# Two attentions in one planned program: input loads, order of the first projections, and the rules of the planner

## The chip, the core and the metric

The kernel runs on one core of a Trainium2 chip. The metric is device time in microseconds (us) of one execution; several executions of the same kernel are compared by their median. One core has five instruction streams that run beside each other and wait for each other by semaphores: TensorE (PE, matmuls; its weight loads are listed apart as PEld), VectorE (DVE), ScalarE (ACT), GpSimd (POOL) and SyncE (SP, which only issues DMAs here). ScalarE and GpSimd issue DMAs too. PE writes its results to PSUM, which has eight banks of 128 partitions x 512 float32.

## The reference

Two attentions over 2048 tokens with 16 heads of 28 numbers; their outputs stand side by side.

```python
def _A_ref(x, wq, wk, wv, wo):          # one key and one value head for all 16 query heads
    q = (x @ wq).reshape(B, S, H, Dh).transpose(0, 2, 1, 3)
    k = x @ wk
    v = x @ wv
    scores = einsum("bhqd,bkd->bhqk", q, k) * Dh ** -0.5
    o = einsum("bhqk,bkd->bhqd", softmax(scores), v)
    return o.transpose(0, 2, 1, 3).reshape(B, S, H * Dh) @ wo

def _B_ref(x, wqkv, wo):                # each query sees 8 keys: itself and 7 before it, two apart
    q, k, v = heads of x @ wqkv
    logits = q . k[pos - 2 * (0..7)] * Dh ** -0.5, masked where the position is below 0
    return (softmax(logits) . v) @ wo

return concatenate([A, B], axis=-1)     # A_x, B_x: 1 x 2048 x 448, all bfloat16
```

Attention A is the large part: 16 heads x 2048 queries x 2048 keys, each score with an exponential.

## The kernel before

**Work.** Queries of A are taken 512 at a time (four chunks `sc`) and heads four at a time (four groups `g`), which makes 16 groups. Keys are taken 128 at a time (16 blocks `tb`). A job is one head's scores of one key block against 512 queries: one matmul (L1512) into one PSUM bank. A group has 16 x 4 = 64 jobs, and A has 1024. Four heads sit in four row strips of the PE array (28 numbers and a row of ones each), so up to four jobs of one batch run side by side.

**Two ways to the exponential.** Most banks go to ScalarE: one ACTIVATE with Exp (L1250) reads two or three neighbouring banks and writes bfloat16 to `P`. The banks 0 to 2 and 3 to 4 are two rings that take turns, so a batch has three or two of these jobs. Other jobs go to VectorE ("D jobs"): a TENSOR_SCALAR (L1560) turns the bank's scores into int16 that, read as bfloat16, are about the exponential; two more steps on VectorE add 32 to it (L1569, `s1`) and 64 to both (L1576, `s2`), which gives four versions whose weighted sum is the exponential more closely. When two such steps of different jobs are ready together, one instruction does both (`pair`, L1206). A D job therefore has four value matmuls (L1624, operand `Z`, with four scaled copies of the values in `vA`) where a ScalarE job has one (operand `P`). The banks 5 to 7 are called flex: they hold D jobs, the running sums of the value matmuls (one bank for each open group) and the projections ("fills").

**Fills.** Everything else on PE is a fill, a list of steps into one flex bank: the first transposes of A's input, projections of keys (`k0` to `k3`), values and queries of A and B, norms of the queries (whose negative half is added as a further row of the score matmul), B's scores and values in 25-query tiles (L1343, L1310), and output projections (all proj at L661). After a fill an eviction is queued, for VectorE or ScalarE.

**The order is made by a planner in Python**, when the program is built. `_Gen.loop` keeps a planned time for each engine, always lets the engine that is furthest behind choose its next instruction, and adds that instruction's planned duration. PE's choice (`pe_choose`) is between the next batch of scores (`do_qk`), value matmuls (`do_pv`), a fill (`fill_pick`: by due time, if its inputs are planned to be there), a filler matmul (`dummy`, L1707 and L1709) and 20 ns of nothing. The result is a fixed list for each engine. On the chip every engine runs its list in order, and waits for semaphores.

The names that the change touches:

- `xA`, `wA` (`plan_start`): the first 512 tokens of A's input go to `xn`, which lies in `P`; 64 partitions by SP's queue and 64 by ScalarE's. Then the query weights (two DMAs) and the value weights (two) go out on ScalarE's queue and the key weights (two) on SP's, which next issues 12 transposing DMAs for the other three token chunks. The dependencies of the query weights are kept under one name, `wq`.
- `FILL0`, `FILLN` (`want_d`): a D job is wanted only while the number of fills done is at least 124 x (jobs done) / 1024 + `FILL0`; also below a share `DRATE` of D jobs.
- `TWOD`, `RINGD`, `RINGB` (`do_qk`): with `TWOD` a second D job may join a batch of fewer than four jobs if more than one flex bank is free and VectorE's planned backlog is below `RINGB` ns. Where no flex bank is free, and the share of D jobs is below `RINGD` and the backlog below `RINGB`, the third bank of a three-bank ring is read by VectorE instead ("ring D").
- `QKLAT` (`pe_choose`): so many ns before ScalarE runs out of banks the next scores are to be issued. `PRESS`: with so few free `P` slots or fewer, value matmuls go first.
- `HAMTILE` (`step_ready`): B's small tiles are planned only where PE was active for this share of the last 3.4 us of planned time.
- `BDT`: due times of B's four groups are `BT0 + BDT * gg` (us, planned). `VB0`: B's value projections may begin then.
- `quiet`: the broadcast of the reciprocal sums (`d3`, `bc<-rec_scratch`, four DMAs of 64 KB) is issued only where SP's planned time is past the planned end of PE's last instruction fetch (`fetched`; a fetch is counted for every 256 instructions and takes `FTIME`), and more than `FQUIET` instructions are left to the next. Before that come the copy of the sums to `PVs` (L987, five buffers) and `den`, `rec`; after it the product on GpSimd (L1033).
- The score of the first batch needs `kT_A` (keys, evicted by ScalarE, L714) and `qT_A` with its norm row: square on ScalarE (L837), scaled copy on VectorE (L834), norm matmul, sum on VectorE (L762).

Of the kernel before, what the change touches and what calls it, by code (L numbers as in the profile page):

```python
# [5 lines left out]
ACT = mybir.ActivationFunctionType  # L6
# [51 lines left out]
BT0 = 90  # L58
BDT = 36
DRATE = 0.3  # L60
DTAIL = 12
NWARM = 8
QKLAT = 560.0
TOL = 40.0
DWAIT = 200.0
FTOL = 100.0
FSTART = 0.0
TWOD = False
SPARE = 0
# [17 lines left out]
HAMLOW = 0.61  # L87
HAMTILE = 0.54
LATE = 1000.0
RINGD = 0.22  # L90
RINGB = 900.0
PRESS = 1
PV3 = 8
JOBO = 0.0
JOBL = 1.0
XL0 = 4300.0
FILLN = 124.0
FILL0 = 4.0
FRATE = 0.036
FQUIET = 70  # L100
PAIR = True

SCHED = ()
VB0 = 29.0
WO0 = 70
# [98 lines left out]
class _Gen:  # L204
    def __init__(self, nc, A_x, A_wq, A_wk, A_wv, A_wo, B_x, B_wqkv, B_wo, out):
        self.nc = nc
        self.A_x, self.A_wq, self.A_wk, self.A_wv, self.A_wo = A_x, A_wq, A_wk, A_wv, A_wo
        self.B_x, self.B_wqkv, self.B_wo = B_x, B_wqkv, B_wo
        self.out = out
        self.ops = []  # L210
        self.T = {e: 0.0 for e in ("pe", "act", "dve", "gp", "sp")}
        self.mode = None
        self.port = 0.0
        self.pend = []
        self.fills = []
        self.cur = None
        self.actq = []
        self.gprows = None
        self.dport = None
        self.landed = {}  # L220
        self.ninst = 30.0
        self.block = 0
        self.fetched = 0.0
        self.streams = []
        self.work = []
# [76 lines left out]
    def pe_op(self, mode, emit, ns, reads=(), writes=(), appends=(), name="", share=0.93):  # L302
# [12 lines left out]
        if block > self.block:  # L315

            self.block = block
            self.fetched = max(o.start, self.fetched) + FTIME
        self.streams.append((o.start, o.start + ns, share))
        self.work.append((o.start, o.start + ns, share))  # L320
# [179 lines left out]
    def plan_start(self):  # L500
# [7 lines left out]
        def res(*k):  # L508
            if k not in R:
                R[k] = Res()  # L510
            return R[k]
# [8 lines left out]

        def wA(q, t, src, c1, key, lands):
            self.dma_op(q, t[:, 0:3, 0:c1], src[0:384, :].rearrange("(k p) c -> p k c", p=128), writes=[res(key)], lands=lands, name=key)
            self.dma_op(q, t[64:128, 3, 0:c1], src[384:448, :], appends=[res(key)], lands=lands, name=key)

        def xA(q, r, lands):
            self.dma_op(q, g.xn[64 * r:64 * r + 64, :, :], g.A_x[0, 256 * r:256 * r + 256, :].rearrange("(p b) c -> p b c", b=4),
                        writes=() if r else [res("xn")], appends=[res("xn")] if r else (), lands=lands, name="x")
        xA("sp", 0, XL0)
        xA("act", 1, XL0)
        wA("act", g.wq, g.A_wq, D, "wq", 4500.0)  # L530
        wA("sp", g.wk, g.A_wk, DH, "wk", 4000.0)
        wA("act", g.wv, g.A_wv, DH, "wv", 4000.0)

# [5 lines left out]
        for t, c1, key in ((g.wq, D, "wq"), (g.wk, DH, "wk"), (g.wv, DH, "wv")):  # L539
            dve(lambda e, t=t, c1=c1: e.memset(t[0:64, 3, 0:c1], 0.0), 100, writes=[res(key + "0")])  # L540
            dve(lambda e, t=t, c1=c1: e.memset(t[:, :, c1:], 0.0), 80, appends=[res(key + "0")])
        put("act", lambda e: e.activation(g.col[:, 3:4], g.zero[:, 0:1], ACT.Exp, scale=1.0), 1500, 1500, reads=[res("zero")], writes=[res("tl")])
        gp(lambda e: e.memset(g.ident[:, :], 0.0), 200, writes=[res("id0")])
# [25 lines left out]
        for k in range(4):  # L569
# [6 lines left out]
                                     base=DH - 1, pattern=[[32, 4]], channel_multiplier=-1), 200, reads=[res("f2")], writes=[res("sel4")])  # L576
        gp(lambda e: e.memset(g.wB[0:64, 3, :], 0.0), 900, writes=[res("wB0")])
        gp(lambda e: e.memset(g.woA[:, :, :], 0.0), 1600, writes=[res("woA0")])
        gp(lambda e: e.memset(g.woB[:, :, :], 0.0), 1600, writes=[res("woB0")])
# [85 lines left out]
    def make_fills(self):  # L665
# [35 lines left out]
        for c in range(4):  # L701
# [7 lines left out]
            def after(bank, c=c):  # L709
# [3 lines left out]
                if c == 0:  # L713
# [5 lines left out]
                           prio=0.5 if c == 0 else 1, name="ke")  # L719
            fill(f"k{c}", (-84, T0 + 1, T0 + 5, T0 + 10)[c], steps, after, ring=True, enabled=landed if c else None)  # L720

# [126 lines left out]
        for sc in range(4):  # L848
            for gg in range(4):
                due = (-90 if gg == 0 else T0 - 12 + 18 * gg) if sc == 0 else -40 + gg  # L850
                q_fill("A", ("A", sc), sc % 2, gg, g.wq, 4 * gg * DH, g.xT_A, KA, "xA", sc, due, [res("wq"), res("wq0")],
                       (lambda sc=sc: sc == 0 or self.groups_issued >= 4 * sc - AHEAD))
            if sc > 0:
                q_norms("A", ("A", sc), sc % 2, -30)
# [331 lines left out]
    def quiet(self):  # L1186

        return self.T["sp"] >= self.fetched and FBLOCK * (self.block + 1) - self.ninst > FQUIET

# [498 lines left out]
    def dummy(self, T):  # L1688
# [3 lines left out]
        if T < 10000.0:  # L1692
            m, l, r, rd = "full", g.zero[:, 0:128], g.zero[:, 0:448], [self.res("zero")]
        elif self.mode == "row":
            m, l, r, rd = "row", g.wq[0:DH + 1, 0, 0:128], g.wq[0:DH + 1, 1, 0:448], [self.res("wq")]
        else:
            m, l, r, rd = "col", g.wq[0:KA, 0, 0:32], g.wq[0:KA, 1, 0:448], [self.res("wq")]
        for b in self.flex + [3, 4, 0, 1, 2]:
# [118 lines left out]
```

## Time and profile before

| | us |
|---|---|
| median of 12 runs | 399.64 (399.13 to 401.84) |
| the profiled execution | 399.62 |
| its span, from the first to the last instruction | 397.90 |
| first exponential starts | 12.57 |
| last exponential ends | 388.08 |
| last PE instruction of the chain ends | 393.42 |
| GpSimd issues B's weights | 8.59 to 10.1 |
| B's weights are first read | 31.4 |

The profile is of one execution. A span is from the first to the last instruction of the profile, and the execution's own time is a little longer. Busy time of an engine is the time in which at least one of its instructions runs; neighbouring ScalarE instructions overlap in the records, so the mean duration of one is longer than its share of the busy time. The granted clock of PE was 0.999 of full speed. In a line of the groups there stand, in order: the line of the program, the engine, the operation, out<-in with shapes, the count, the busy us and the mean ns of one, then the idle time before these instructions and what ended it.

### The profile page before, as it was taken

Reading aid. Unit: us, or ns where it says so; the run is one execution under the profiler, and the core shown is the slowest. Engines: PE = TensorE matmul, PEld = TensorE weight load, DVE = VectorE, ACT = ScalarE, POOL = GpSimd, SP = SyncE. Lnnn points to the kernel's source line nnn. Section 1 sums busy time; section 2 is a strip of 40 time slices with the busy share of each in tenths; the row PEclk is TensorE's granted clock in tenths of the full one; section 3 lists DMA queues with packets and bytes.
Section 4 is the critical chain, followed back from the end, with each engine's and each line's share of the span. In section 5 each row is a group of like instructions: output and inputs, shape, how many; then the busy total and the mean of one; then the engine's idle time right before and its main releaser. Section 6 shows DMA issues by size and latency. Waiting matters only on the chain.

```text
span 397.9 us, 16416 instructions
## 1 busy us (share of the span) xinstructions
PE 383.8 (96%) x7223; PEld 132.2 (33%) x7223; DVE 361.8 (91%) x812; ACT 380.9 (96%) x374; POOL 61.3 (15%) x81
## 2 busy tenths in 40 slices
PE   7999999999999999999999999999999999999995
PEld 3333223323223343232433333243334433232332
DVE  2887899999999999989989989999999999999954
ACT  2799999999999999999999999999999999999992
POOL 8800001012300020221101021210011211122110
PEclk9999999999999999999999999999999999999999
DMA  7986694234100110312000122000012212224212
GB/s 150 200 106 128 122 171 100 64 82 102 43 6 3 32 33 7 94 37 78 14 4 31 31 56 65 15 20 3 7 44 61 73 27 45 71 61 125 66 48 95
DMA packets 42403, 25.09 MB, mean 63 GB/s; under 512 B 28348, under 2 KB 37740, under 8 KB 42332
## 3 DMA queue, kind: packets, MB, share of 16 engines
q1 hardware_dynamic: 40268, 21.05, 24.6%
q0 software_dynamic: 736, 2.11, 1.9%
q8 instruction: 57, 0.93, 1.0%
q10 hardware_dynamic: 1328, 0.89, 0.9%
q14 instruction: 14, 0.11, 0.1%
HBM read 13.80 MB, written 6.02 MB: 50 GB/s over the span
## 4 chain that ended last, share of the span: by engine, by line
ACT 78%; PE 16%; DVE 3%; DMA 1%; issue 1%; SPq 0%; DVEq 0%
ACT P L1250 76%; PE ps L661 5%; PE ps L1624 5%; PE ps L1512 4%; ACT P L1366 2%; DMA wk<-in_A_wk_dram 1%; DVE Z L1560 1%; PE ps L1343 1%; DVE xT_A L1089 1%; PE ps L1310 0%; SPq L334 0%; DVE Z L1206 0%; DVE Z L1576 0%; DVE sq L1089 0%; DVE qT_A L834 0%
## 5 line engine op out<-in xcount | busy, mean ns | idle before, releaser
L1250 ACT ACTIVATE P<-ps 128x1536 bf16<-128x1536 f32 (+1 forms) x349 | 372.3, 1327 | 2.1 <-PE ps L1512 2.1
L1560 DVE TENSOR_SCALAR Z<-ps 128x512 int16<-128x512 f32 x215 | 146.3, 683 | 8.2 <-PE ps L1512 7.1
L1512 PE MATMUL ps<-qT_A,kT_A 29*128 29x512 bf16 x1024 | 136.4, 384 | 5.4 <-ACT P L1250 2.6
L1624 PE MATMUL ps<-P,vA 128*32 128x512 bf16 x809 | 140.3, 385 | 0.0
L1624 PE MATMUL ps<-Z,vA 128*32 128x512 bf16 x860 | 139.2, 385 | 0.2
L1512 PEld LDWEIGHTS ps<-qT_A,kT_A 29*128 29x128 bf16 x1024 | 35.3, 91 | 127.9 <-ACT P L1250 74.4
L1206 DVE TENSOR_SCALAR Z<-Z 128x1024 int16<-128x1024 int16 (+1 forms) x96 | 52.1, 554 | 0.3
L1033 POOL TENSOR_TENSOR oTn<-PVs,bc 128x512 bf16<-128x512 f32 x15 | 19.2, 1283 | 207.3 <-DVE Z L1576 77.5
L1576 DVE TENSOR_SCALAR Z<-Z 128x1024 int16<-128x1024 int16 x115 | 48.7, 426 | 0.8
L1624 PEld LDWEIGHTS ps<-P,vA 128*32 128x32 bf16 x809 | 34.5, 94 | 32.3 <-issue 21.7
L1624 PEld LDWEIGHTS ps<-Z,vA 128*32 128x32 bf16 x860 | 33.3, 94 | 29.9 <-issue 19.2
L661 PE MATMUL ps<-xT_B,wB 128*32 128x512 bf16 x512 | 40.2, 382 | 0.1
L1569 DVE TENSOR_SCALAR Z<-Z 128x512 int16<-128x512 int16 x123 | 35.1, 295 | 0.7
L1033 POOL TENSOR_TENSOR oTnB<-PVs,bc 128x512 bf16<-128x512 f32 x16 | 20.4, 1273 | 96.0 <-DVE Z L1569 30.0
L987 DVE COPY PVs<-ps 128x512 f32<-128x512 f32 x31 | 21.0, 678 | 0.7 <-PE ps L1624 0.6
L661 PE MATMUL ps<-xT_A,wq 128*32 128x512 bf16 x256 | 20.4, 383 | 0.4 <-DVE qT_A L840 0.4
L661 PE MATMUL ps<-wB,xT_B 128*32 128x448 bf16 x256 | 18.0, 355 | 0.0
L661 PE MATMUL ps<-woA,oTn 128*32 128x448 bf16 x256 | 17.4, 355 | 0.0
L661 PE MATMUL ps<-woB,oTnB 128*32 128x448 bf16 x256 | 17.0, 356 | 0.0
L661 PEld LDWEIGHTS ps<-xT_B,wB 128*32 128x32 bf16 x512 | 11.4, 95 | 13.2 <-issue 7.7
L1310 PE MATMUL ps<-P,vB 32*32 32x25 bf16 (+1 forms) x1344 | 15.5, 171 | 0.1
L1343 PE MATMUL ps<-qT_B,kT_B 29*32 29x25 bf16 (+1 forms) x1344 | 14.9, 172 | 0.2 <-issue 0.2
(98 smaller groups left out, 231.2 us busy)
## 6 DMA issues: line engine op xcount, KB each, us to landing
bc<-rec_scratch SPq DMA_DIRECT2D x124, 64.0 KB, 2.0
v_scratch<-kT_B SPq DMA_DIRECT2D x16, 128.0 KB, 1.8
out_dram<-xT_A SPq DMA_DIRECT2D x15, 112.0 KB, 1.7
out_dram<-sq SPq DMA_DIRECT2D x15, 112.0 KB, 2.0
vB<-v_scratch SPq DMA_DIRECT2D x2, 640.0 KB
vB<-v_scratch SPq DMA_DIRECT2D x2, 608.0 KB
wB<-in_B_wqkv_dram POOLq DMA_DIRECT2D x1, 1008.0 KB, 7.6
den<-PVs SPq DMA_DIRECT2D x31, 8.0 KB
```

Of the source, the lines that this page charges most:

```text
L661: ins = e.matmul(self.bank(bank, 32 * j, 32 * j + m, 0, n), lhs(j), rhs(j), start=start, stop=stop, tile_position=(0, 32 * j))
L987: return dict(emit=lambda e: e.tensor_copy(out=g.PVs[:, p, :], in_=g.bank(bank.i)), reads=[bank.res], writes=[self.pvs.res[p]], took=ns + ...
L1033: return dict(emit=lambda e: e.tensor_tensor(out=dst(z), in0=g.PVs[:, p, :], in1=g.bc[:, b, :], op=ALU.mult), reads=[self.pvs.res[p], self ...
L1206: op = self.put("dve", lambda e: e.tensor_scalar(out=self.Z[:, sl, v1:v1 + n, :], in0=self.Z[:, sl, v0:v0 + n, :], scalar1=1.0, scalar2=ad ...
L1250: op = self.put("act", lambda e: e.activation(g.P[:, 1536 * k:1536 * k + 512 * n], g.ps[:, lo:lo + 512 * n], ACT.Exp, scale=ASCALE), ns, n ...
L1310: ins = e.matmul(g.bank(bank, 32 * j, 32 * j + 32, q0, n), g.vB[32 * c:32 * c + 32, b, 4 * gg + j, :], g.P[32 * c:32 * c + 32, x:x + n], s ...
L1343: ins = e.matmul(g.bank(bank, 32 * c, 32 * c + 32, q0, n), g.kT_B[32 * j:32 * j + DH + 1, s, k0:k0 + 32], g.qT_B[32 * j:32 * j + DH + 1, s ...
L1512: ins = e.matmul(g.bank(b), g.kT_A[32 * j:32 * j + DH + 1, 128 * tb:128 * tb + 128], g.qT_A[32 * j:32 * j + DH + 1, gr.sc % 2, gr.g, :], s ...
L1560: return dict(emit=lambda e: e.tensor_scalar(out=g.Z[:, z, 0, :], in0=g.bank(bank.i), scalar1=ZBIAS, scalar2=0.0, op0=ALU.add, op1=ALU.max ...
L1569: return dict(emit=lambda e: e.tensor_scalar(out=g.Z[:, z, 1, :], in0=g.Z[:, z, 0, :], scalar1=1.0, scalar2=32.0, op0=ALU.mult, op1=ALU.ad ...
L1576: return dict(emit=lambda e: e.tensor_scalar(out=g.Z[:, z, 2:4, :], in0=g.Z[:, z, 0:2, :], scalar1=1.0, scalar2=64.0, op0=ALU.mult, op1=AL ...
L1624: ins = e.matmul(g.bank(b, 32 * j, 32 * j + 32), l, r, start=st, stop=sp, tile_position=(0, 32 * j))
```

## The change

Nothing of what is computed changes. In the planner's start:

- The first input is split by token blocks (`b` 0 and 1, `b` 2 and 3; a partition holds four tokens) instead of by partitions, still one half for each of the two queues.
- The query weights come in two parts, with a dependency each: columns 0 to 127 (those of the first group of heads) behind the input on ScalarE's queue, the rest behind ScalarE's first activation, which loads the table. The value weights move from ScalarE's queue to GpSimd's, behind the clearing of `wB`.
- The first key projection `k0` is enabled only after the first query projection.

In the rules: the gate for the broadcasts compares with a time `fetching` (1.9 us earlier than `fetched`) and asks for 90 instructions left, 135 while a B tile is under way; `TWOD` is on; and further constants change.

```diff
-BDT = 36
+BDT = 37
-QKLAT = 560.0
+QKLAT = 600.0
-TWOD = False
+TWOD = True
-HAMTILE = 0.54
+HAMTILE = 0.56
-RINGD = 0.22
-RINGB = 900.0
-PRESS = 1
+RINGD = 0.25
+RINGB = 1200.0
+PRESS = 2
-XL0 = 4300.0
+XL0 = 3600.0
-FILL0 = 4.0
+FILL0 = 6.0
-FQUIET = 70
+FQUIET = 90
-VB0 = 29.0
+VB0 = 25.0
...
             self.fetched = max(o.start, self.fetched) + FTIME
+            self.fetching = self.fetched - FTIME + 1500.0
...
-        def xA(q, r, lands):
-            self.dma_op(q, g.xn[64 * r:64 * r + 64, :, :], g.A_x[0, 256 * r:256 * r + 256, :].rearrange("(p b) c -> p b c", b=4),
-                        writes=() if r else [res("xn")], appends=[res("xn")] if r else (), lands=lands, name="x")
-        xA("sp", 0, XL0)
-        xA("act", 1, XL0)
-        wA("act", g.wq, g.A_wq, D, "wq", 4500.0)
-        wA("sp", g.wk, g.A_wk, DH, "wk", 4000.0)
-        wA("act", g.wv, g.A_wv, DH, "wv", 4000.0)
+        def wA(q, t, src, c0, c1, rs, lands, issue=560.0):
+            self.dma_op(q, t[:, 0:3, c0:c1], src[0:384, c0:c1].rearrange("(k p) c -> p k c", p=128), writes=[rs], issue=issue, lands=lands, name="wA")
+            self.dma_op(q, t[64:128, 3, c0:c1], src[384:448, c0:c1], appends=[rs], issue=issue, lands=lands, name="wA")
+        def xA(q, b0, b1, lands):
+            self.dma_op(q, g.xn[:, b0:b1, :], g.A_x[0, 0:512, :].rearrange("(p b) c -> p b c", b=4)[:, b0:b1, :],
+                        writes=[res("xn")] if b0 == 0 else (), appends=[res("xn")] if b0 else (), lands=lands, name="x")
+        xA("sp", 0, 2, XL0)
+        xA("act", 2, 4, XL0)
+        wA("act", g.wq, g.A_wq, 0, 128, res("wq", 0), 3500.0)
+        wA("sp", g.wk, g.A_wk, 0, DH, res("wk"), 3900.0)
...
-        put("act", lambda e: e.activation(g.col[:, 3:4], g.zero[:, 0:1], ACT.Exp, scale=1.0), 1500, 1500, reads=[res("zero")], writes=[res("tl")])
+        put("act", lambda e: e.activation(g.col[:, 3:4], g.zero[:, 0:1], ACT.Exp, scale=1.0), 1300, 1300, reads=[res("zero")], writes=[res("tl")])
+        wA("act", g.wq, g.A_wq, 128, D, res("wq", 1), 3500.0)
...
         gp(lambda e: e.memset(g.wB[0:64, 3, :], 0.0), 900, writes=[res("wB0")])
+        wA("gp", g.wv, g.A_wv, 0, DH, res("wv"), 3500.0, 700.0)
         gp(lambda e: e.memset(g.woA[:, :, :], 0.0), 1600, writes=[res("woA0")])
...
-            fill(f"k{c}", (-84, T0 + 1, T0 + 5, T0 + 10)[c], steps, after, ring=True, enabled=landed if c else None)
+            fill(f"k{c}", (-84, T0 + 1, T0 + 5, T0 + 10)[c], steps, after, ring=True, enabled=landed if c else lambda: self.q0done)
...
-                q_fill("A", ("A", sc), sc % 2, gg, g.wq, 4 * gg * DH, g.xT_A, KA, "xA", sc, due, [res("wq"), res("wq0")],
+                q_fill("A", ("A", sc), sc % 2, gg, g.wq, 4 * gg * DH, g.xT_A, KA, "xA", sc, due, [res("wq", 0), res("wq0")] + ([res("wq", 1)] if gg else []),
...
     def quiet(self):
-        return self.T["sp"] >= self.fetched and FBLOCK * (self.block + 1) - self.ninst > FQUIET
+        short = self.cur is not None and self.cur.list[self.cur.i][0] == "tile" or any(f.list[f.i][0] == "tile" for f in self.parked)
+        return self.T["sp"] >= self.fetching and FBLOCK * (self.block + 1) - self.ninst > FQUIET * (1.5 if short else 1.0)
```

The filler matmuls, which read `wq`, name both of its parts now.

## The prediction

> **What bounds the kernel now.** I read the busy times first, then the windows by stage, then the chain of waits, then the groups by form, then the DMA issues. The page's first block, and three windows (length, then busy time and count on PE, weight load, VectorE, ScalarE, GpSimd):
>
> ```profile
> PE 383.8 (96%) x7223; PEld 132.2 (33%) x7223; DVE 361.8 (91%) x812; ACT 380.9 (96%) x374; POOL 61.3 (15%) x81
> 0.00:12.57 12.57, 9.65 (x96) 3.91 (x96) 4.59 (x25) 3.37 (x5) 10.94 (x30) 1.00 0.80 176
> 80.00:120.00 40.00, 39.57 (x567) 11.84 (x568) 39.70 (x85) 40.00 (x40) 6.67 (x10) 1.00 0.25 58
> 12.57:388.00 375.43, 368.80 (x7026) 125.76 (x7025) 352.42 (x780) 375.39 (x365) 50.32 (x52) 1.00 0.27 58
> 40.00:388.00 348.00, 342.49 (x6640) 116.70 (x6632) 329.99 (x721) 347.97 (x341) 44.65 (x39) 1.00 0.22 53
> ```
>
> The time has three parts: 12.57 us until the first exponential, 375.43 us in which ScalarE never rests (375.39 busy), and 397.90 - 388.00 = 9.90 us of tail. ScalarE sets the middle, but VectorE has only 348.00 - 329.99 = 18.0 us idle between 40 and 388, and PE 375.43 - 368.80 = 6.6 us. The groups by form, with mean ns:
>
> ```profile
> L1250 ACT ACTIVATE P<-ps 128x1024 bf16<-128x1024 f32 x238 | 251.9, 1194 | 0.0
> L1250 ACT ACTIVATE P<-ps 128x1536 bf16<-128x1536 f32 x111 | 178.7, 1610 | 2.1 <-PE ps L1512 2.1
> L1560 DVE TENSOR_SCALAR Z<-ps 128x512 int16<-128x512 f32 x215 | 146.3, 683 | 8.2 <-PE ps L1512 7.1
> L1576 DVE TENSOR_SCALAR Z<-Z 128x1024 int16<-128x1024 int16 x115 | 48.7, 426 | 0.8
> L1569 DVE TENSOR_SCALAR Z<-Z 128x512 int16<-128x512 int16 x123 | 35.1, 295 | 0.7
> L1206 DVE TENSOR_SCALAR Z<-Z 128x2048 int16<-128x2048 int16 x50 | 34.2, 684 | 0.3
> L1206 DVE TENSOR_SCALAR Z<-Z 128x1024 int16<-128x1024 int16 x46 | 18.8, 413 | 0.0
> ```
>
> ScalarE takes 238 x 2 + 111 x 3 = 809 of the 1024 score banks, VectorE 215, a share of 0.21. The mean durations overlap; what a bank costs ScalarE follows from the difference of the two forms, 1.610 - 1.194 = 0.42 us, and from (375.43 - 16 x 0.49 for the B exponentials) / 809 = 0.454 us, which includes the share of a whole instruction. A bank on VectorE costs 0.683 + 0.295 + 0.426 = 1.40 us alone, or 0.683 + (0.413 + 0.684) / 2 = 1.23 us when its two steps are done in pairs.
>
> The start, in the chain of waits (start, length), and two DMA issues with the time to landing:
>
> ```profile
> 2.33 5.10 DMA wk<-in_A_wk_dram
> 7.43 0.09 issue
> 7.53 0.61 PE ps L661 x8
> 8.14 0.29 PE ps L1709
> 8.44 1.44 PE ps L661 x24
> 9.87 0.02 issue
> 9.90 0.61 ACT sq L837
> ...
> 10.53 0.76 DVE qT_A L834
> ...
> 11.39 0.70 DVE qT_A L762
> ...
> 12.13 0.42 PE ps L1512 x3
> ...
> 12.57 1.45 ACT P L1250
> ```
>
> ```profile
> P<-in_A_x_dram SPq DMA_DIRECT2D x1, 224.0 KB, 4.6
> P<-in_A_x_dram ACTq DMA_DIRECT2D x1, 224.0 KB, 3.5
> ```
>
> The keys' weights land at 7.43, the keys' 16 matmuls run, then the queries' 16, and only the queries have the long rest of the way: square, scale, norm, score, 2.70 us from 9.87 to 12.57.
>
> **Queries ahead of keys.** The last transposed input is ready at 7.19 (ScalarE's copy, 6.59 + 0.60). The queries can start at 7.25 and need 16 x (1.44 / 24) = 0.96 us, so they end at 8.2 instead of 9.87: -1.6 us. The links after them keep their length. The keys now run 8.2 to 9.2, and the norm's matmul, ready at 8.9, waits behind them until 9.2; but the addition L762 also needs the scaled queries, at 8.9 + 0.76 = 9.65, so that wait is hidden by 0.05 to 0.1 us. The keys' eviction on ScalarE (0.69) ends near 9.9, before the score at 10.5. The keys' weights at 7.43 stop nothing any more.
>
> **Input by halves of tokens.** The halves land at 0.81 + 3.5 = 4.3 and 0.80 + 4.6 = 5.4, and the transposes start at 5.47 with the later. The new halves are as large, with all partitions each. Bounds: both at the mean, 4.85, -0.55; or 0.4 later, since the pieces are twice as many. I take -0.2, because less than a third of the query weights (114 of 392 KB) now travels beside them. [...]
>
> **Query weights in two parts.** The first part is two issues on ScalarE's queue in place of the whole, so as many as before. It needs to be there at 7.25; it lands between the input (5.4) and the 7.43 of the keys' weights, which travel in smaller pieces: at worst +0.2. [...] The second part adds two issues (1.14 us) behind the table load. With the values' issues gone, the load can begin at about 2.6 instead of 3.77 and ScalarE is free at about 5.2, before its copy at 6.59; cover 1.4 us. The part lands at 5.2 + 3.5 to 5.1 = 8.7 to 10.3, and group 1 of the queries wants it about 9.8, ahead of the first score on PE: 0 to +0.5, taken 0.
>
> **Value weights on GpSimd.** Two issues between the clearing L577 (ends 5.43) and L578, at the 0.75 us of the wB issues: 1.5 us. They hold up woA, woB, the ones, wB (8.59 to about 10.1), the masks. wB lands 7.6 later, at 17.7, and is first read at 31.4, or some 4 us earlier with VB0 = 25: cover 9 us. If the cover were gone, PE would wait in its order for the whole rest. The values are first needed after the first norm, at about 9; issued by 7.0, they land at 8.7 to 10; up to +0.4 if late, taken 0 because the values' fill can move behind a score.
>
> Start in all: -1.6 - 0.2 = **-1.8 us**, between -2.6 and -0.6. What is late next? 16 jobs of the first four key blocks last 16 / 2.5 x 1.14 us = 7 us, to about 18; the second key chunk was evicted by 15.9. So the start's gain stays.
>
> **Two banks per batch, RINGD, RINGB.** More score banks may go to VectorE: 0.43 us off ScalarE each. RINGD did not bind before (0.21 against 0.22), so RINGB (1200 against 900 ns of VectorE backlog) and the second bank must do it. Bounds: none, or all of VectorE. In its best window (80 to 120) VectorE idles 0.8%; at that, 18.0 - 2.8 = 15.2 us are left, and each job takes 1.3 and shortens the window by 0.43: 9 jobs; if half of the 123 and 115 unpaired steps also became pairs (0.085 us each, 10 us), 15. I take the middle of 94.8% (329.99 / 348.00) and 99.2%, 97%: 2.2% of 348 us = 7.7 us, 6 jobs: 6 x 0.43 = **-2.6 us**, between 0 and -6.5. PE pays 3 more value matmuls per job, 18 in all, 1 us (four at a time in 0.22 us) to 3 us (0.167 each); it has 6.6 us idle and 25 sets of filler matmuls (L1707, some 0.2 each), so this is hidden as long as the window shrinks by less than some 8 us.
>
> **The other constants** (QKLAT, HAMTILE, PRESS, FILL0, BDT, FQUIET, the broadcasts' gate) reorder work: 0. Broadcasts against instruction fetch can win at most the 6.6 us PE idle, and no single wait of its weight loads there is over 0.7 us. If broadcasts wait longer, the five PV buffers cover it; without that cover a flex bank stays taken. The last B group falls due 3 us later; the tail I leave at 9.90, give or take 0.8.
>
> **Sum.** 397.90 - 1.8 - 2.6 = 393.5 span, plus 399.62 - 397.90 = 1.72 around it: **395.2 us**. The profiled run (399.62) is the median (399.64) within 0.02.
>
> **Rivals.** (A) The second bank is seldom found, because three flex banks also hold sums and fills; the share stays at 0.21 and only the start is won: 399.62 - 1.8 = 397.8. For it: the share never reached the old limit. Against: RINGB's looser limit acts without a flex bank. (B) VectorE fills up with better pairs, 15 jobs: 399.62 - 1.8 - 6.5 = 391.3. For it: 99% in one window; against: 92 to 93% between 160 and 240, where the pace of the fills, not the backlog, may ration. (C) Slower: VectorE works in order, and a second bank puts 0.68 us ahead of every eviction behind it (projection banks, PV copies); PE, in order too, then waits at a score whose bank is not free, and ScalarE starves for the first time. From 4.4 / 0.68 = 7 such batches on the path the gain is gone; with 10, 399.62 - 4.4 + 6.8 = 402.0. For it: VectorE at 95%, PE idle only 6.6 us; against: the backlog limit holds for the second bank too. (D) Start gain and stalls cancel: 399.6.
>
> **How the numbers follow.** The forecast (393.8 to 396.6) has 0.40, A 0.18, B 0.16, C 0.21, D 0.05. About 0.2% (0.8 us) is what a measurement can tell from no change. Faster: 0.40 + 0.18 + 0.16 = 0.74; same 0.05; slower 0.21. The range runs from 390.8 (B with its 0.5) to 400.8, where it takes in A and D and the mild end of C; beyond it lie some 0.16 of C and 0.03 of B.
>
> **What would show it.** The first exponential near 10.8; queries' matmuls before keys'; L1560 near 221; fewer L1250 (347 or less); VectorE 97% between 40 and 388; a tail near 10. It is wrong if the start's DMAs land later than 7.5, if ScalarE shows idle time between exponentials, or if L1560 falls below 210.

## The result, and the profile after

The changed kernel takes **398.47 us** (median of 12 runs, 397.27 to 399.04) where the kernel before takes 399.53 us (50 runs). The ratio is 0.9969, with an interval of 0.9960 to 0.9979: faster by 0.3%, or 1.1 us. The sign was forecast; the size was not, since 4.4 us had been forecast. Here and below a ratio compares runs taken side by side on one chip, so it can differ a little from the quotient of the two medians.

The profiled execution took 398.17 us. First the windows of the kernel after (length, then busy time and count on PE, weight load, VectorE, ScalarE, GpSimd; granted clock, DMA share, GB/s), cut where its first exponential starts and its last one ends (the last row is the stretch that was shown of before):

```profile
0.00:10.41 10.41, 7.82 (x72) 3.23 (x72) 4.13 (x22) 3.37 (x5) 9.04 (x25) 1.00 0.82 152
10.41:387.39 376.98, 369.85 (x7029) 126.71 (x7028) 350.41 (x765) 376.82 (x367) 53.40 (x59) 1.00 0.26 60
40.00:388.00 348.00, 341.81 (x6630) 117.25 (x6622) 328.66 (x709) 347.24 (x341) 44.59 (x39) 1.00 0.21 53
```

The first window is 2.16 us shorter than its counterpart of before (12.57). But between 40 and 388 VectorE, which had 329.99 us of work, now has 328.66: it was not given more, it was given less. ScalarE is as full as before, for 376.82 of 376.98 us, and has more to do. The groups by form of the kernel after (busy us and mean ns of one, then idle time before):

```profile
L1255 ACT ACTIVATE P<-ps 128x1024 bf16<-128x1024 f32 x242 | 255.6, 1206 | 0.1
L1255 ACT ACTIVATE P<-ps 128x1536 bf16<-128x1536 f32 x109 | 176.9, 1623 | 1.2 <-PE ps L1517 1.1
L1565 DVE TENSOR_SCALAR Z<-ps 128x512 int16<-128x512 f32 x213 | 144.4, 683 | 11.7 <-PE ps L1517 10.6
...
L1211 DVE TENSOR_SCALAR Z<-Z 128x2048 int16<-128x2048 int16 x57 | 40.3, 710 | 0.2
...
L1211 DVE TENSOR_SCALAR Z<-Z 128x1024 int16<-128x1024 int16 x52 | 22.5, 441 | 0.0
```

D jobs went from 215 to 213, so ScalarE reads 811 banks in 351 instructions, where it read 809 in 349. The pairs rose from 96 to 109, and what they saved VectorE was not spent. The chain of waits of the kernel after, at the start (start, length, what):

```profile
1.74 4.85 DMA wq<-in_A_wq_dram
6.59 0.04 issue
6.63 1.08 PE ps L665 x16
7.71 0.02 issue
7.73 0.61 ACT sq L841
...
8.36 0.76 DVE qT_A L838
...
9.22 0.70 DVE qT_A L766
...
9.97 0.41 PE ps L1517 x3
```

It begins with the queries' weights; their 16 matmuls run at once, and square, scale, norm and score follow with the lengths they had. The same chain at the end:

```profile
387.81 3.19 PE ps L665 x63
...
391.46 0.54 ACT xT_A L1091
```

In the chain of before there stood in this place:

```profile
388.51 4.89 PE ps L661 x99
```

After the last exponential 63 output projections stand in the chain now, where there were 99 before. The span in parts, from the two profiled executions:

| | before | after | forecast change | change |
|---|---|---|---|---|
| until the first exponential | 12.57 | 10.41 | -1.8 | -2.16 |
| first exponential to the end of the last | 375.51 | 376.98 | -2.6 | +1.47 |
| tail | 9.82 | 8.81 | 0, give or take 0.8 | -1.0 |
| span | 397.90 | 396.20 | -4.4 | -1.7 |

The medians differ by less (1.1) than these two executions (1.45 in their own times, 399.62 and 398.17).

### The profile page after: what moved, and what is told of

Read it like the earlier page. It is cut to its first block, busy times and chain, and to the rows that moved or that the text cites. A ratio compares the mean times of both kernels' runs of the same rounds, so it can differ in the third digit from the quotient of the medians.

```text
span 396.2 us, 16318 instructions
## 1 busy us (share of the span) xinstructions
PE 381.8 (96%) x7178; PEld 132.2 (33%) x7178; DVE 358.1 (90%) x793; ACT 382.2 (96%) x376; POOL 62.4 (16%) x83
## 4 chain that ended last, share of the span: by engine, by line
ACT 67%; PE 23%; DVE 6%; DMA 3%; issue 1%; ACTq 0%; DVEq 0%
ACT P L1255 64%; PE ps L1629 8%; PE ps L1517 7%; PE ps L665 7%; DVE Z L1565 2%; ACT P L1371 2%; DMA den<-PVs 1%; DMA wq<-in_A_wq_dram 1%; DVE Z L1211 1%; DVE kT_B L887 1%; PE ps L1315 0%; DVE Z L1581 0%; DVE Z L1574 0%; DVE PVs L991 0%; DVE sq L1093 0%
## 5 line engine op out<-in xcount | busy, mean ns | idle before, releaser
L1565 DVE TENSOR_SCALAR Z<-ps 128x512 int16<-128x512 f32 x213 | 144.4, 683 | 11.7 <-PE ps L1517 10.6
L1629 PE MATMUL ps<-Z,vA 128*32 128x512 bf16 x852 | 141.1, 385 | 0.5 <-DVE Z L1581 0.2
L1211 DVE TENSOR_SCALAR Z<-Z 128x2048 int16<-128x2048 int16 (+1 forms) x109 | 61.9, 582 | 0.2
L1629 PEld LDWEIGHTS ps<-Z,vA 128*32 128x32 bf16 x852 | 34.1, 94 | 31.0 <-issue 19.3
L1581 DVE TENSOR_SCALAR Z<-Z 128x1024 int16<-128x1024 int16 x99 | 41.6, 421 | 0.8
L665 PE MATMUL ps<-xT_B,wB 128*32 128x512 bf16 x512 | 39.2, 382 | 0.3 <-DVE kT_B L917 0.3
L1574 DVE TENSOR_SCALAR Z<-Z 128x512 int16<-128x512 int16 x109 | 30.1, 288 | 0.3
L665 PE MATMUL ps<-woA,oTn 128*32 128x448 bf16 x256 | 19.2, 356 | 0.3 <-issue 0.3
```

The costliest lines, as they stand in the source:

```text
L665: ins = e.matmul(self.bank(bank, 32 * j, 32 * j + m, 0, n), lhs(j), rhs(j), start=start, stop=stop, tile_position=(0, 32 * j))
L1211: op = self.put("dve", lambda e: e.tensor_scalar(out=self.Z[:, sl, v1:v1 + n, :], in0=self.Z[:, sl, v0:v0 + n, :], scalar1=1.0, scalar2=ad ...
L1565: return dict(emit=lambda e: e.tensor_scalar(out=g.Z[:, z, 0, :], in0=g.bank(bank.i), scalar1=ZBIAS, scalar2=0.0, op0=ALU.add, op1=ALU.max ...
L1574: return dict(emit=lambda e: e.tensor_scalar(out=g.Z[:, z, 1, :], in0=g.Z[:, z, 0, :], scalar1=1.0, scalar2=32.0, op0=ALU.mult, op1=ALU.ad ...
L1581: return dict(emit=lambda e: e.tensor_scalar(out=g.Z[:, z, 2:4, :], in0=g.Z[:, z, 0:2, :], scalar1=1.0, scalar2=64.0, op0=ALU.mult, op1=AL ...
L1629: ins = e.matmul(g.bank(b, 32 * j, 32 * j + 32), l, r, start=st, stop=sp, tile_position=(0, 32 * j))
```

## The experiments

My theory after the result: the start gained what was forecast (and 0.4 us more), and the rest of the change did not give VectorE more banks; it only dealt the planner's list anew. The rivals: the start's gain is lost again by itself; PE or VectorE, not ScalarE, sets the time; one of the constants carries a gain or a loss of its own.

### One part of the change at a time

**e1_start_only** has the edits of the start and every constant and rule of before; **e2_rules_only** has the constants and rules and the old start. **e3_hamtile_back** and **e4_one_bank** are the kernel after with one constant put back; **e5_start_gate** is the new start with the new gate for broadcasts.

```diff
 e1: -BDT 37, QKLAT 600, TWOD True, HAMTILE 0.56, RINGD 0.25, RINGB 1200, PRESS 2, FILL0 6, FQUIET 90, VB0 25, new gate
     +BDT 36, QKLAT 560, TWOD False, HAMTILE 0.54, RINGD 0.22, RINGB 900, PRESS 1, FILL0 4, FQUIET 70, VB0 29, old gate
 e2: the reverse, beside the old start
 e3: -HAMTILE = 0.56
     +HAMTILE = 0.54
 e4: -TWOD = True
     +TWOD = False
 e5: e1 with the new quiet() and FQUIET = 90
```

> The start as changed, all rules and constants as before. The list that comes out has 211 VectorE banks (before 215, changed kernel 213). Theory 1 (the start's 2.16 us reach the end, banks cost ScalarE 0.45 us each): first exponential at 10.4, middle 4 x 0.45 = 1.8 us longer, end about 0.4 us under the time before, 399.1, give or take the tail. Theory 2 (the end follows PE, which only shifts): the whole 2.2 us, 397.3. Theory 3 (the rules brought the gain): 399.5.

> All rules and constants as changed, the start as before. The list has 225 VectorE banks, 10 more than before, which is more than the prediction's 6. Theory 1 (each bank is worth 0.43 us at the end): 399.5 - 4.3 = 395.2. Theory 2 (what ScalarE saves, PE has still to do: B's output projections move behind the last exponential): last exponential some 4 us earlier, but a tail that is 10 to 20 us longer, 406 to 416.

> The changed kernel with HAMTILE back at 0.54. The list has 220 VectorE banks, 7 more than the changed kernel. Theory 1 (0.43 us each at the end): 398.4 - 3.0 = 395.4. Theory 2 (PE's leftover moves to the tail): last exponential 2 to 3 us earlier than 387.4, end 4 to 7 us later than the changed kernel, 402 to 405.

> The changed kernel with one VectorE bank per batch as before; the second bank was used in 2 batches only. 212 VectorE banks against 213. Theory 1 (the second bank matters by its banks): 398.4 + 0.45 = 398.9. Theory 2 (only the order that comes out matters): anything within 2 us of 398.4, and the sign says nothing of the second bank.

> The changed start and, of the rules, the new gate for the broadcasts alone; all other constants as before. 215 VectorE banks as before. Theory 1 (start gain and banks): first exponential at 10.4, banks as before, so 399.6 - 2.2 = 397.4. Theory 2 (the gate brings nothing by itself): as the start alone, 399.0, give or take the 1 to 4 us that any new order costs or wins.

Measured, with the parts of each profiled execution (D jobs, the length from the first exponential to the end of the last, and the tail behind it):

| | time, us | ratio to before | first exp. | D jobs | middle | tail |
|---|---|---|---|---|---|---|
| before | 399.53 | 1 | 12.57 | 215 | 375.5 | 9.8 |
| after | 398.47 | 0.9969 (0.9960 to 0.9979) | 10.41 | 213 | 377.0 | 8.8 |
| e1_start_only | 398.99 | 0.9984 (0.9976 to 0.9993) | 10.44 | 211 | 377.4 | 9.4 |
| e2_rules_only | 413.14 | 1.0359 (1.0312 to 1.0405) | 12.70 | 225 | 371.2 | 27.0 |
| e3_hamtile_back | 405.46 | 1.0141 (1.0127 to 1.0155) | 10.69 | 220 | 374.7 | 18.0 |
| e4_one_bank | 402.85 | 1.0087 (1.0071 to 1.0102) | 10.17 | 212 | 377.8 | 11.9 |
| e5_start_gate | 398.66 | 0.9986 (0.9973 to 1.0000) | 10.08 | 215 | 378.8 | 8.8 |

Four readings. The start alone (e1) wins 2.1 us at the first exponential and 0.6 us in all: with the same constants the planner now finds 211 jobs for VectorE, not 215, and the middle is 1.9 us longer (4 x 0.43 = 1.7 by my price of a bank). The rules alone (e2) give VectorE ten jobs more, and the middle is 4.3 us shorter, as my price per bank had it (10 x 0.43); but the tail is 17 us longer. So the same rules that end with 213 jobs beside the new start end with 225 beside the old one. One constant among ten (e3: 7.0 us) weighs more than the whole change. And the new gate for the broadcasts is worth nothing that e5 can tell from e1. The intervals of e1 and of the kernel after overlap slightly, so that the last 0.5 us between these two are barely told apart.

Whether e2's tail is matmuls or waits is read from its chain of waits, behind the last exponential at 383.90:

```profile
388.05 2.53 DMA bc<-rec_scratch
390.59 0.07 issue
390.65 1.28 POOL oTnB L1035
391.94 0.04 issue
391.98 2.64 PE ps L663 x52
...
399.69 2.02 DMA bc<-rec_scratch
...
402.23 1.33 POOLq L389
403.56 0.04 issue
403.60 2.67 PE ps L663 x52
```

Twice a broadcast of reciprocal sums lands, GpSimd multiplies, and PE projects one of B's last groups. Those groups had not been finished under the exponentials.

### Which engine sets the time

In these three the order of every instruction is that of before; only the work of one engine's instructions shrinks. e6 leaves out the last 16 of 512 columns of nearly all exponentials, e7 the last 320 of 448 columns of B's output projections, e8 the last 64 of 512 columns of the first VectorE step of most D jobs.

```diff
 e6_light_scalar
-  e.activation(g.P[...512 * n], g.ps[...512 * n], ACT.Exp, scale=ASCALE)
+  e.activation(g.P[...][:, :, 0:w], g.ps[...][:, :, 0:w], ACT.Exp, scale=ASCALE)        # w = 496
 e7_light_pe
-  lambda j, t=t: wo[:, t, :], D, start=(t == 0), stop=(t == 3)
+  lambda j, t=t: wo[:, t, 0:128] if kind == "B" else wo[:, t, :], 128 if kind == "B" else D, ...
 e8_light_vector
-  e.tensor_scalar(out=g.Z[:, z, 0, :], in0=g.bank(bank.i), ...)
+  e.tensor_scalar(out=g.Z[:, z, 0, 0:w], in0=g.bank(bank.i)[:, 0:w], ...)               # w = 448
```

> The kernel before, every instruction in the same place, but nearly all of attention A's exponentials on ScalarE leave out the last 16 of 512 columns of each bank: some 780 banks x 16 x 0.83 ns = 10 us less work for ScalarE. Theory 1 (ScalarE sets the middle, as predicted): 399.6 - 9 to 10 = 390. Theory 2 (PE's list sets the pace, ScalarE is fed just in time): 396 to 399.

> The kernel before, every instruction in the same place, but B's output projections multiply 128 instead of 448 columns: 64 steps x 320 / 2.4 ns = 8.5 us less for PE, of which 16 steps (2 us) lie behind the last exponential. Theory 1 (PE has cover): 399.6 - 2 = 397.5. Theory 2 (PE's list sets the pace): 392 to 395.

> [...] Theory 1 (VectorE has 18 us idle and sets nothing): 399.6, at most 1 us less. Theory 3 (VectorE's evictions hold up PE): 5 us or more less.

Measured: e6 392.49 us (0.9829, 0.9816 to 0.9841), 7.1 us less for an estimated 10.4 us of columns taken away (16 columns x 809 banks x the planner's 0.833 ns, less the few that stay whole; in the windows ScalarE's busy time falls by 7.6 us); e7 399.28 us (1.0003, 0.9991 to 1.0014) for 8.5 us of matmul columns (the busy time of these projections falls from 17.0 to 8.5 us); e8 399.52 us (1.0008, 0.9995 to 1.0020) for 11.7 us on VectorE (the busy time of the first steps falls from 146.3 to 134.6 us; 191 of them take 620 ns in place of 683). The windows of the three, e6 between its own first and last exponential, the others in the window of before:

```profile
12.70:381.46 368.76, 364.77 (x7026) 126.13 (x7025) 349.25 (x781) 367.82 (x365) 50.18 (x52) 1.00 0.28 60
```

```profile
12.57:388.00 375.43, 364.09 (x7030) 124.60 (x7025) 352.28 (x781) 375.20 (x365) 50.03 (x52) 1.00 0.26 59
```

```profile
12.57:388.00 375.43, 368.70 (x7034) 124.53 (x7029) 344.23 (x781) 375.22 (x365) 50.39 (x52) 1.00 0.27 59
```

With PE 11.3 us idle (e7) or VectorE 31.2 us idle (e8), ScalarE is as full as before and the time stands. In a fixed order ScalarE is the only one of the three that sets the time up to the last exponential. That part of my reading of the profile holds. But e7 did not win the 2 us that were expected behind the last exponential either. PE is busy there with these projections for 1.25 us instead of 3.38, and the tail of the profiled execution is only 0.2 us shorter (9.62 us). Its chain now passes through VectorE, which finishes the last group of A:

```profile
390.33 0.72 DVE oTn L978
391.06 0.04 issue
391.10 0.97 PE ps L661 x16
```

### The start

e9 splits the first input by partitions again, inside the kernel after; e10 makes the first part of the query weights three times as wide; e11 puts the first keys ahead of the queries (its middle and tail came out in another order, so that only its start is compared).

```diff
 e9_x_partitions
-  g.xn[:, b0:b1, :], g.A_x[0, 0:512, :].rearrange("(p b) c -> p b c", b=4)[:, b0:b1, :]
+  g.xn[32 * b0:32 * b1, :, :], g.A_x[0, 128 * b0:128 * b1, :].rearrange("(p b) c -> p b c", b=4)
 e10_wq_384
-  wA("act", g.wq, g.A_wq, 0, 128, ...)   wA("act", g.wq, g.A_wq, 128, D, ...)
+  wA("act", g.wq, g.A_wq, 0, 384, ...)   wA("act", g.wq, g.A_wq, 384, D, ...)
 e11_keys_first
-  wA("sp", g.wk, ..., 3900.0)   fill(f"k{c}", (-84, ...)[c], ..., enabled=landed if c else lambda: self.q0done)
+  wA("sp", g.wk, ..., 2600.0)   fill(f"k{c}", (-92, ...)[c], ..., enabled=landed if c else None)
```

> The changed kernel, every instruction in the same place, but the first input again as two halves of 64 partitions. If the halves by tokens brought the input earlier: first transposes at about 5.0 instead of 4.4 and the first exponential up to 0.6 us later than 10.4, end 0.6 us later. If the shape of the halves is nothing and only the fewer bytes beside them count: 4.4, 10.4 and 398.5 as the changed kernel.

> The changed kernel, every instruction in the same place, but the first part of the query weights has 384 of 448 columns instead of 128 (three times the bytes, rows of 768 instead of 256 bytes). If bytes set the landing: the queries' first matmul at 7.5 or later instead of 6.6, and the first exponential some 1 us later, 11.4. If the short rows cost as much as the bytes saved: no later than 10.4.

> The changed kernel with the key projection put ahead of the first queries again (the list after the start is a new one, with a long planned tail, so only the start is compared). If the order is worth its 16 matmuls and the breaks beside them: first exponential 1.0 to 1.6 us later than 10.4, near 11.7. If the earlier landings made the gain: 10.4 to 10.7.

Measured: e9 398.37 us (0.9986, 0.9968 to 1.0004 of the kernel before on its chip), first exponential at 10.51; e10 398.24 us (0.9970, 0.9957 to 0.9983), at 10.61; e11 428.39 us in one run, at 11.79. PE's timeline of e11 (start, length):

```profile
6.60 0.75 PE L665 MATMUL ps<-xT_A,wk 128*32 128x512 bf16 x8
7.28 0.36 PE L1714 MATMUL ps<-Z 128*128 128x448 bf16 x1
7.58 0.61 PE L665 MATMUL ps<-xT_A,wk 128*32 128x512 bf16 x8
8.02 1.04 PE L665 MATMUL ps<-xT_A,wq 128*32 128x512 bf16 x16
```

The queries start at 8.02 where after has 6.63, and the first exponential comes 1.38 us later: so the order is worth 1.4 of the 2.16 us. Both are single executions. In the ten profiles of this study that have the new order and the input split by tokens (e10 among them) the first exponential comes between 10.08 and 10.69, so the 1.4 could be 1.1 to 1.7. The split of the input shows in PE's timeline of e9:

```profile
5.54 1.05 PE L685 MATMUL ps<-ident,P 128*128 128x128 bf16 x16 [0.87 <-POOL wB L580]
6.44 0.36 PE L1714 MATMUL ps<-Z 128*128 128x448 bf16 x1
6.73 1.05 PE L665 MATMUL ps<-xT_A,wq 128*32 128x512 bf16 x16
```

and in that of the kernel after:

```profile
4.40 1.05 PE L685 MATMUL ps<-ident,P 128*128 128x128 bf16 x16
...
6.63 1.05 PE L665 MATMUL ps<-xT_A,wq 128*32 128x512 bf16 x16 [0.97 <-DMA wq<-in_A_wq_dram]
```

The transposes begin 1.1 us sooner with the split by tokens, but the queries only 0.1: in the kernel after they wait 0.97 us for their weights. (The releaser in e9's first line is a GpSimd clearing that no transpose needs; by the DMA issues the half on SyncE's queue lands 4.6 us after its issue there, and 3.2 in after.) The 1.1 us are no accident of one execution: in the eleven profiles of this study with token halves the transposes begin between 4.40 and 4.80, in the six with partition halves between 5.50 and 5.72. The 0.1 us are less than executions differ: in the ten profiles just named the queries begin between 6.30 and 6.86, and e9's 6.73 lies among them. So a gain of the split by itself is not shown.

e9 also shows where the other 0.8 of the 2.16 us lie. Its transposes are as late as before's (5.54 and 5.50), yet its first projection starts at 6.73, right behind them, where that of before waited for the keys' weights until 7.53. And e11's keys start at 6.60. So the weights that are needed first are there sooner. Whether the smaller first part of the query weights or the value weights' move to another queue brings this, no run separates.

A second bound lies close by, in e1's chain of waits:

```profile
1.25 3.59 PE ps L610 x8
4.84 1.70 PE ps L685 x16
6.54 0.19 PE ps L1713
6.73 1.00 PE ps L665 x16
```

Here PE is never idle: its filler matmuls and transposes last until 6.73 by themselves, because the same 16 transposes take 1.70 us, not 1.05. They run at 0.11 us each in place of 0.07. Of the eleven early starts nine have such slow transposes (1.39 to 1.91 us), of the six late ones none slower than 1.29. e10 is one of the nine:

```profile
4.84 1.71 PE ps L685 x16
6.55 0.35 PE ps L1714
6.90 1.01 PE ps L665 x16
```

That its first exponential comes 0.2 us later than after's is therefore not the price of the wider weights: PE goes from the transposes through a filler matmul to the queries without a wait, so that three times the bytes cost nothing that shows. Input, weights, and transposes that can take 0.11 us each in place of 0.07 all end near 6.6 (the weights at 6.59 in the kernel after, the transposes at 6.54 in e1 and 6.55 in e10), and speeding one of them alone can win little.

### The planner's price of an exponential

If each choice of constants deals another list, the question is whether a better list is to be had. The planner charges an exponential 52 ns and 0.833 ns a column. The profile of before gives, if the planner's price of a column (512 x 0.833 ns = 0.4266 us a bank) is right, (375.43 - 16 x 0.49 - 809 x 0.4266) / 349 = 0.064 us in place of the 52 ns; with the 0.416 us a bank by which the two forms of before differ (1610 and 1194 ns) it would be 0.089. e12 and e13 charge 64 and take other constants, without and with the second bank; e14 takes other constants with the old 52. e15 is e3 with B's output projections cut to 128 of 448 columns, to see what its tail is made of.

```diff
 e12_true_exp      EXP0 52 -> 64, BT0 90 -> 88, DWAIT 200 -> 150, TWOD True -> False, FSAFE 300 -> 400,
                   HAMTILE 0.56 -> 0.50, RINGB 1200 -> 1000, PV3 8 -> 6, FQUIET 90 -> 70
 e13_true_exp_two  EXP0 52 -> 64, BDT 37 -> 36, QKLAT 600 -> 620, DWAIT 200 -> 150, HAMTILE 0.56 -> 0.52,
                   RINGD 0.25 -> 0.22, PV3 8 -> 7, FQUIET 90 -> 80, VB0 25 -> 29, WO0 70 -> 60
 e14_old_exp       HAMTILE 0.56 -> 0.50, FQUIET 90 -> 60
 e15_hamtile_light e3, with wo[:, t, 0:128] for kind "B"
```

> The changed start, with the planner's fixed time of an exponential at the 64 ns that the profile gives instead of 52, so that PE has more planned room between scores, and other constants chosen with it (one VectorE bank per batch). 218 VectorE banks and 345 exponentials, 5 and 6 off the changed kernel. Theory A (a new order wins by fewer banks on ScalarE, if the fills still fit before the last exponential): last exponential near 385.0, tail 9 us, 395.7 to 396.5. Theory B (any order lands where chance puts it): 398 to 403.

> As the run with the true time of an exponential, but with the second VectorE bank and a different choice of the other constants; 218 VectorE banks, 347 exponentials. Theory A: 396 to 397. Theory B: 398 to 403. If the second bank were a gain in itself: under the run with one bank.

> The changed kernel with HAMTILE at 0.50 and FQUIET at 60, the best planned end that was found with the planner's old 52 ns; 216 VectorE banks, 352 exponentials. The planner ends it 0.6 us before the changed kernel. Theory A: 3 banks x 0.45 less 1 exponential: 397.5. Theory B: 398 to 403.

> The order of the HAMTILE run (405.5 us, tail 18 us), every instruction in the same place, but B's output projections multiply 128 instead of 448 columns (their results are incomplete). 56 of their 64 steps lie behind the last exponential in the list. If that tail is PE's left-over work: 56 x 0.133 = 7.4 us less, 398. If the tail is waits for evictions and DMAs: 404 to 405.5.

Measured: e12 397.35 us (0.9943, 0.9927 to 0.9959), e13 397.14 us (0.9930, 0.9916 to 0.9945; four runs), e14 399.29 us (1.0000, 0.9980 to 1.0019), e15 403.83 us (1.0107, 1.0094 to 1.0120). **e13 and e12 beat both kernels**: the intervals of both lie below that of the kernel after. e13 is a little outside the 396 to 397 of theory A, e12 lies between its two theories, and e14 is where theory B had it. The groups of e13:

```profile
L1255 ACT ACTIVATE P<-ps 128x1024 bf16<-128x1024 f32 x235 | 243.9, 1155 | 1.2 <-PE ps L1517 0.9
L1255 ACT ACTIVATE P<-ps 128x1536 bf16<-128x1536 f32 x112 | 176.7, 1578 | 3.0 <-PE ps L1517 2.8
L1565 DVE TENSOR_SCALAR Z<-ps 128x512 int16<-128x512 f32 x218 | 147.8, 682 | 8.5 <-PE ps L1517 7.1
```

Here 218 banks go to VectorE and 806 to ScalarE in 347 instructions, with a tail of 8.7 us that is no longer than after's: it and e12 (218 banks, a tail of 8.6 us) are the first lists that have the banks without the tail. ScalarE pays for it with some 3 us of waits for scores (1.2 + 3.0 in these rows, of which the wait for the first score is a part). The profiled execution (398.35 us) was the slowest of e13's four (the others 396.19 to 397.24), and e12's (397.84 us) lies above its median too. In both the stretch from the first exponential to the end of the last (377.8 and 377.2 us) is no shorter than after's 377.0, so where the gain of their medians comes from is not shown. Nor is the price shown as its cause: e12 and e13 change eight and nine other constants with it, no run changes the price alone, and e14, one list at the old price, does not settle it against a lucky deal.

e3's tail in its chain of waits, and SyncE's timeline of e15 (the issues of output transfers):

```profile
389.08 9.86 PE ps L665 x204
398.94 0.02 issue
398.97 0.62 DVE xT_A L1093
```

```profile
390.56 2.88 SPq L336 DMA_DIRECT2D out_dram<-sq  x4
...
393.97 3.26 SPq L336 DMA_DIRECT2D out_dram<-sq  x4
397.28 1.45 SPq L336 DMA_DIRECT2D out_dram<-xT_A  x3
```

In e3 204 output projections run behind the last exponential, twice as many as before. But taking 320 of the 448 columns from B's projections shortens the kernel by 1.6 us (1.4 by the two ratios), not by the 6.2 that PE's part behind the last exponential shrinks (10.9 to 4.7 us for 224 matmuls): in e15 PE's last projection ends at 394.3, and the output transfers are issued on SyncE, one behind another, until 398.7. A block of output left behind the last exponential costs its matmuls, its eviction and its place in SyncE's queue, and the last two did not shrink here (an eviction takes 0.54 us on ScalarE and 0.62 on VectorE in e3 and in e15).

## Why the prediction was right or wrong

**Queries ahead of keys**: right. Forecast -1.6; the order measured alone (e11) is 1.4 (1.1 to 1.7) of the 2.16 us. The links behind the queries kept their lengths, and the keys' matmuls and eviction delayed nothing, as worked out.

**Input by halves, weights in two parts**: -0.2 forecast, the other 0.8 measured. I had taken the transposes from 5.47 to 5.27; they came at 4.40, and the queries at 6.63, not 7.25. Averaging the landings of before was wrong. But the earlier input by itself gains nothing that shows (0.1 in e9, less than executions differ), because the weights then end last (6.59 in the kernel after), or the transposes take up to 1.91 us in place of 1.05; the 0.8 us are weights that land earlier, the term to which I had given "at worst +0.2". Whether the first part's short rows cost anything, no run here shows: e10, with pieces of 768 bytes in place of 256, was held up by PE and not by its weights. Nor does a run show the "0.4 later" that I had feared for twice as many pieces: the halves by tokens, two transfers on the same two queues as the halves by partitions, were in use 1.1 us earlier.

**Two banks per batch, RINGD, RINGB**: this is the step that failed. "6 jobs: 6 x 0.43 = -2.6 us" became 2 jobs fewer, and +1.47 us: ScalarE is busy for 376.82 us in place of 375.48, which two banks (0.9), two more exponentials (0.13) and B's 16 (12.7 us in place of 12.4) make up; another 0.1 are waits. I sized the term by the idle time of VectorE, as if a looser limit would fill it. Even so it was sized too high: I divided 7.7 us by 1.3 a job and left out the 0.43 by which each job shortens the window, which I had counted for the 9 jobs; with it there are 4.5 jobs, -1.9 us. What the planner meets, batch by batch, when it deals the two lists:

| batches | before | after |
|---|---|---|
| with a D job in a flex bank | 152 | 145 |
| with a ring D | 63 | 66 |
| no free `Z` buffer (there are six) | 15 | 28 |
| no free flex bank, and no ring D either | 101 | 97 |
| of these, three-bank batches refused for a backlog above RINGB (900, then 1200 ns) | 57 | 39 |
| no D job wanted, or none that fits | 18 | 15 |

Flex banks, VectorE's planned backlog and `Z` buffers rationed the jobs, and the looser rules moved only the second. A second bank was taken in 2 batches: of the 101 batches of after that had a D job and room for another, 99 found only one flex bank free, and the two that found a second took it. That is the reason that rival A gives. And RINGB did bind: 19 of the ring D jobs were taken at a planned backlog above the old 900 ns. But their number rose only from 63 to 66, while the jobs in flex banks fell by 7 and the batches without a `Z` buffer rose by 13. That the ring D jobs hold the buffers that the others then lack fits these counts; it is not shown, and e2, with the same rules beside the old start, has 225 jobs. RINGD and FILL0 bind nowhere: with their old values the same list comes out. Nor does the new condition on `k0`: the queries go first because the planner has their weights land ahead of the keys'. I had named the doubt (rival A, 397.8 us, the share stays at 0.21: it is 213 / 1024 = 0.208) and gave it 0.18; the result is 0.7 us above it. That it came so near is in part luck: the middle's +1.47 was met by a tail 1.0 us shorter and a start that gained 0.4 us more than forecast. That a flex bank is wanted by sums and fills was for it, and should have weighed more than the "best window" of 40 us.

**The other constants: 0**. Wrong as a rule, though near in sum. They are not edits with an effect of their own: each new value deals the list again, and the lists of this study lie between 397.1 and 413.1 us, e11's apart. The whole change is the start alone (0.9984) and some 0.5 us of another deal, which the two intervals barely tell apart.

**The tail: 9.90, give or take 0.8**. It was 8.81 here, but 27.0, 18.0 and 11.9 in e2, e3 and e4. I costed more D jobs as "PE pays 3 more value matmuls per job", hidden in its idle time. Where they were hidden, fills went out of the middle: of the first five lists e2 and e3, with the most D jobs and the shortest middles (371.2 and 374.7), have the longest tails. Had the forecast's 221 jobs come, this step might have failed in its turn; but it need not, since e12 and e13 have 218 jobs and tails of 8.6 and 8.7.

**What bounds the kernel**: right in a fixed order (e6 to e8). Rival C's mechanism, ScalarE waiting for scores, did not show in the kernel after (0.16 us idle between the first and the last exponential), but the deal of e5 has it, where 215 banks on VectorE won nothing. Its window from the first exponential to the end of the last, in an execution of 399.46 us, 0.8 above e5's median, has ScalarE idle for 2.8 us:

```profile
10.08:388.89 378.81, 369.29 (x7054) 126.91 (x7053) 351.43 (x796) 376.03 (x365) 53.89 (x60) 1.00 0.27 60
```

## What to carry to other kernels

Where a planner deals a list, a constant has no price: ask first whether the rule binds (how often the second bank is found, which resource refuses), and count the jobs of the changed list rather than the idle time of an engine. Work that is moved off the engine in front must be paid by another that also has to clear its own work before the end; look at the tail for it (in e2 the middle was 4.3 us shorter and the tail 17 us longer). Where three things end together at the start, speeding one of them wins little, but the order of what follows them can win its full length (here some 1.4 us).

## What was not expected of the hardware

- An exponential in an unbroken stream costs ScalarE, by an estimate from the 375.43 us, 809 banks and 349 exponentials of before, about 64 ns beside its columns at the planner's price of a column, and 89 ns at the 0.416 us a bank by which the two forms differ; the planner has 52. At 64 ns that is some 4.3 us over 349 of them that the planned time lacked.
- PE's pace in the first microseconds differs between the profiled executions: 16 transposes that begin between 4.4 and 4.8 take 1.05 us in two profiles and 1.39 to 1.91 in nine, that is 0.07 us each in the kernel after (last matmul's length included) and 0.11 in e1. The granted clock reads 1.00 alike in the start windows of the kernel after (0.07) and of e1 and e10 (0.11); what makes the difference, no run here shows. In nine of eleven executions the earlier input met slower transposes.
- Three times the bytes in the first piece of weights (336 in place of 112 KB, e10) were not waited for: PE was busy without a gap until their first use.
- The window of before had PE busy for 368.80 of 375.43 us, and taking 8.5 us of matmul columns out of it (e7) changed the time by no more than 0.14% (ratio 0.9991 to 1.0014).
